# In one batch of a fused attention and channel MLP kernel, the x of two tiles made two slots later, behind the next batch's scores

## The chip, the cores and the metric

The kernel runs on one core of one Trainium2 chip. The metric is the device time of one execution in microseconds (us). The kernel before takes 257.06 us (median of 3 runs, 256.99 to 257.06). TensorE (PE) does the matmuls, VectorE (DVE) and ScalarE (ACT) empty the accumulators and do the element-wise work, GpSimd (POOL) makes some sums and issues loads. All runs told of here were in the fast state, with a granted TensorE clock of 0.99 to 1.00.

## The reference, cut to what matters

```python
a = softmax(phi)                      # 8 batches, 8 heads, 576 rows, 32 memories
k_m, v_m = a^T k, a^T v               # per head, 32 x 64
attn = softmax(q k_m^T / 8)
x  = (attn v_m), heads side by side   # 8 x 576 x 512
xn = (x - mean) / sqrt(var + 1e-6) * g_ln
out = x + relu(xn @ w_ch1) @ w_ch2    # w_ch1 512 x 2048, w_ch2 2048 x 512
```

The kernel doesn't normalise x before the first product. It multiplies w_ch1 with v_m once a batch ("w1b"), takes the mean out there, and applies 1/sqrt(var) ("rstd") at the very end. So x of a tile is needed only for its statistics and for the last addition, and there is some freedom as to when it is made.

## The kernel before

Two batches make a pair of 1152 rows, which is nine tiles of 128 rows. The even batch ends with tiles 0 to 3, the odd one with tiles 4 to 8. The parts that matter, shortened:

```python
def big(...):  return psum.tile(..., tag="big", bufs=3)     # three accumulators, in rotation
def one(...):  return psum.tile(..., tag="one", bufs=2)     # two accumulators: second product

def x_tiles(pr, ts):             # x of one or two tiles
    o_ps = big(...);             # matmuls from Eh and vb, 8 for tiles 6 and 7
    nc.scalar.activation(out=x, in_=o_ps, func=AF.Copy)              # ACT
    for i in range(n): bn_stats(x), bn_aggr -> mv                    # DVE

def x_rstd(pr, ts):
    rstd = Ln(var + eps); rstd = Exp(-0.5 * rstd)                    # ACT, waits for mv

def a_den(b, finish=True):       # denominators of the next batch's softmax
    den = big(...); matmuls; rd = Ln(den)                            # PE, ACT
    if finish: a_den2(b)         # rd = Exp(-rd) on ACT; Eh = E * rs * rd on DVE

def mm2(pr, t, j0, j1):          # second product of tile t, accumulator from one()
    ...
    if j1 == JC: mm2_out(pr, t)  # DVE: x = ch_ps * rstd + x; then the store

for b in range(1, B):
    mm1(b, 0, JC)                # h of this batch, 64 matmuls
    ex = {...}                   # slot 2i+half: what runs behind that half of tile i
    ...
    ex[1] += [lambda: a_tr(nb)]                    # kvT of the next batch
    ex[1] += [lambda: x_tiles(pr, t1)]             # t1 = tiles 6, 7 in an odd batch
    ex[2] += [a_sum(nb), a_w1b(nb, 0), a_w1b(nb, 1)]
    ex[2] += [lambda: x_rstd(pr, t1)]
    ex[3] += [lambda: a_sc(nb)]                    # scores of the next batch
    if odd: ex[4] += [lambda: x_tiles(pr, t2), lambda: x_rstd(pr, t2)]   # t2 = tile 8
    ex[3] += [a_vb(nb)]
    ex[4] += [a_den(nb)]
    ex[6 if odd else 5] += [a_w1b(nb, 2), a_w1b(nb, 3)]
    ...
    for i, t in enumerate(tiles):
        for half in range(2):
            mm2(pr, t, 8 * half, 8 * (half + 1))
            for f in ex[2 * i + half]: f()
```

The schedule is manual: each engine executes in the order in which the code names its instructions.

The softmax here doesn't subtract the row's maximum and nothing guards it: scores larger than these inputs give would overflow.

Of the kernel before, what the change touches and what calls it, by code (L numbers as in the profile page):

```python
# [16 lines left out]
def kernel(  # L17
# [38 lines left out]
    def big(shape, dtype, name):  # L56
        return psum.tile(shape, dtype, name=name, tag="big", bufs=3)
# [38 lines left out]
    def load(b):  # L96
        loaded[b] = (phis[b] if b > 2 else load_phi(b, nc.gpsimd), load_kv(b), load_q(b))
# [81 lines left out]
    def a_exp(b):  # L179
        phi_st, kv, q_bf = loaded[b]  # L180
        e = att.tile([P, NS, 4, M], BF16, name="e_sb")
        nc.scalar.activation(out=e.rearrange("p c j m -> p j c m"),  # L182
                             in_=phi_st.rearrange("p j (c m) -> p j c m", m=M), func=AF.Exp)
        st8[b] = {"e": e, "kv": kv, "q": q_bf}
        if b >= 2:
            es = att.tile([P, P], FP32, name="es")
            ev = e.rearrange("p c j m -> p c (j m)")
            a4 = att.tile([P, 4, P], FP32, name="es4", bufs=1)
            nc.gpsimd.tensor_tensor(out=a4, in0=ev[:, 0:4], in1=ev[:, 4:8], op=ALU.add)  # L189
            a2 = att.tile([P, 2, P], FP32, name="es2", bufs=1)  # L190
            nc.gpsimd.tensor_tensor(out=a2, in0=a4[:, 0:2], in1=a4[:, 2:4], op=ALU.add)
            nc.gpsimd.tensor_tensor(out=es, in0=a2[:, 0], in1=a2[:, 1], op=ALU.add)
            nc.gpsimd.tensor_tensor(out=es, in0=es, in1=ev[:, 8], op=ALU.add)
            hl = att.tile([P, 2, P], BF16, name="hl")
            nc.gpsimd.tensor_copy(out=hl[:, 0], in_=es)
            nc.gpsimd.tensor_tensor(out=hl[:, 1], in0=es, in1=hl[:, 0], op=ALU.subtract)
            st8[b]["es"] = hl
# [37 lines left out]
    def a_kv(b):  # L235
        ps = big([P, 2, 512], FP32, "kv_ps")
        kv_mm(b, ps, slice(0, 2))
        if b < 2:
            kv_sum(b, ps)
            rs_out(b, ps)  # L240
        k_out(b, ps, True)
        v_out(b, ps[:, :, D:2 * D])
# [59 lines left out]
    def a_sc(b):  # L302
        s = st8[b]
        kvT, qT = s["kvT"], s["qT"]
        E_ = att.tile([P, 2, 2 * HP], BF16, name="E_sb", bufs=1)
        for g in range(2):
            sc = big([P, 2, 512], FP32, "sc_ps")
            for j in range(4):
                for r in range(2):
                    nc.tensor.matmul(  # L310
                        sc[32 * j:32 * (j + 1), r, 0:HP],
                        kvT[64 * r:64 * (r + 1), g, 32 * j:32 * (j + 1)],
                        qT[64 * r:64 * (r + 1), j, :, TS * g:TS * (g + 1)],
                        start=True, stop=True, tile_position=(64 * r, 32 * j))
            nc.scalar.activation(out=E_[:, g].rearrange("p (a x) -> p a x", a=2),  # L315
                                 in_=sc[:, :, 0:HP], func=AF.Exp, scale=s["rs"][:, g:g + 1])
        s["E"] = E_
# [46 lines left out]
    def mm1(b, j0, j1):  # L364
        s = st8[b]
        if b % 2 == 0 and j0 == 0:
            pair[b // 2] = moe.tile([P, JC, 2 * S], BF16, name="rT", bufs=1)
        rT = pair[b // 2]
        off = S * (b % 2)
        for j in range(j0, j1):  # L370
            h_ps = big([P, 2, 512], FP32, "h_ps")
            for g in range(2):
                for half in range(2):
                    nc.tensor.matmul(  # L374
                        h_ps[:, half, 0:HS], s["w1b"][:, g, P * j:P * (j + 1)],
                        s["Eh"][:, g, HS * half:HS * (half + 1)],
                        start=(g == 0), stop=(g == 1))
            dst = rT[:, j, off:off + S].rearrange("p (a x) -> p a x", a=2)
            if j % 3 or j == 0:
                nc.scalar.activation(out=dst, in_=h_ps[:, :, 0:HS], func=AF.Relu)  # L380
            else:
                nc.vector.tensor_scalar(out=dst, in0=h_ps[:, :, 0:HS], scalar1=0.0, scalar2=None,  # L382
                                        op0=ALU.max)
# [3 lines left out]
    def x_tiles(pr, ts):  # L387
        n = len(ts)
        o_ps = big([P, 2, 512], FP32, "o_ps")
        for i, t in enumerate(ts):  # L390
            parts = []
            lo = P * t
            while lo < P * (t + 1):
                bb = lo // S
                hi = min(P * (t + 1), S * (bb + 1))
                parts.append((2 * pr + bb, lo - S * bb, hi - S * bb, lo - P * t))
                lo = hi
            for (b, a, z, po) in parts:
                s = st8[b]
                for g in range(2):  # L400
                    for u in range(2):
                        r = 64 * u
                        ov = o_ps[po:po + z - a, u, 256 * i:256 * (i + 1)]
                        nc.tensor.matmul(  # L404
                            ov.rearrange("p (j e d) -> p j e d", e=2, d=D)[:, :, g, :],
                            s["Eh"][r:r + 64, g, a:z],
                            s["vb"][r:r + 64, g, 2 * u:2 * (u + 1), :].rearrange("p j d -> p (j d)"),
                            start=True, stop=True, tile_position=(r, po))
        x = moe.tile([P, 2, C], FP32, name="x_sb", bufs=4)
        nc.scalar.activation(out=x[:, 0:n].rearrange("p i (u y) -> p i u y", u=2),  # L410
                             in_=o_ps.rearrange("p u (i y) -> p i u y", i=2)[:, 0:n],
                             func=AF.Copy)
        mv = moe.tile([P, 2, 2], FP32, name="mv", bufs=4)
        for i in range(n):
            stt = moe.tile([P, 6], FP32, name="bst", bufs=4)
            nc.vector.bn_stats(out=stt, in_=x[:, i, :])  # L416
            nc.vector.bn_aggr(out=mv[:, i, :], in_=stt)  # L417
        for i, t in enumerate(ts):
            xs[(pr, t)] = (x[:, i, :], mv, i, n)

    def x_rstd(pr, ts):
        _, mv, _, n = xs[(pr, ts[0])]
        rstd = moe.tile([P, 2], FP32, name="rstd", bufs=4)
        nc.scalar.activation(out=rstd[:, 0:n], in_=mv[:, 0:n, 1], func=AF.Ln, bias=eps_sb)  # L424
        nc.scalar.activation(out=rstd[:, 0:n], in_=rstd[:, 0:n], func=AF.Exp, scale=-0.5)
        for t in ts:
            x, _, i, _ = xs[(pr, t)]
            xs[(pr, t)] = (x, rstd[:, i:i + 1])
# [123 lines left out]
    for b in range(1, B):  # L552
        pr = b // 2
        mm1(b, 0, JC)
        odd = b % 2
        tiles = [4, 5, 6, 7, 8] if odd else [0, 1, 2, 3]
        t1, t2 = tiles[2:4], tiles[4:5]
        nb = b + 1
        if b > 1:
            x_rstd(pr, tiles[0:2])  # L560
        ex = {i: [] for i in range(2 * len(tiles))}
        if nb < B:
            ex[0] += [lambda: a_exp(nb), lambda: a_qT(nb, 0), lambda: a_kv(nb)]
            if nb + 1 < B:
                ex[0] += [lambda: phis.update({nb + 1: load_phi(nb + 1)})]
            ex[1] += [lambda: a_tr(nb)]
        if b == 1:
            ex[0] += [lambda: x_tiles(0, [4, 5]), lambda: x_rstd(0, [4, 5])]
        ex[1] += [lambda: x_tiles(pr, t1)]
        if nb < B:  # L570
            ex[2] += [lambda: a_sum(nb), lambda: a_w1b(nb, 0), lambda: a_w1b(nb, 1)]
        ex[2] += [lambda: x_rstd(pr, t1)]
        if nb < B:
            ex[3] += [lambda: a_sc(nb)]
        if odd:
            ex[4] += [lambda: x_tiles(pr, t2), lambda: x_rstd(pr, t2)]
        if nb < B:
            ex[3] += [lambda: a_vb(nb)]
            ex[4] += [lambda: a_den(nb)]
            ex[6 if odd else 5] += [lambda: a_w1b(nb, 2), lambda: a_w1b(nb, 3)]  # L580
            ex[8 if odd else 6] += [lambda: x_tiles(nb // 2, [4, 5] if nb % 2 else [0, 1])]
            if nb + 1 < B:
                ex[7] += [lambda: load(nb + 1)]
        for i, t in enumerate(tiles):
            if b == B - 1 and t == tiles[-1]:
                mm2_last(pr, t)
                continue
            for half in range(2):
                mm2(pr, t, 8 * half, 8 * (half + 1))
                for f in ex[2 * i + half]:  # L590
                    f()
# [30 lines left out]
```

## Time and profile before

| of the profile before (span 254.5 us) | value |
|---|---|
| PE busy | 95% of the span |
| DVE, ACT busy | 61%, 51% |
| batch 1, from the first kv matmul of batch 2 to the first h matmul of batch 2 | 64.11 to 85.67, 21.56 us |
| from there to the end of the span | 168.8 us |
| granted clock | 1.00 |

Busy shares are of recorded instructions, and the end of a matmul is modelled; so I read starts. Below, "the stretch" is the third row. It contains everything that the change moves. One record of a matmul can be missing: the profile before shows seven of the eight second products that open the stage, so I don't start the stretch there. In the timeline the columns are start, duration, engine and line, out<-in, shapes, count, and in brackets the idle time of the engine before it and who ended it.

### The profile page before, as it was taken

Reading aid. Unit: us, or ns where it says so; the run is one execution under the profiler, and the core shown is the slowest. Engines: PE = TensorE matmul, PEld = TensorE weight load, DVE = VectorE, ACT = ScalarE, POOL = GpSimd, SP = SyncE. Lnnn points to the kernel's source line nnn. Section 1 sums busy time; section 2 is a strip of 40 time slices with the busy share of each in tenths; the row PEclk is TensorE's granted clock in tenths of the full one; section 3 lists DMA queues with packets and bytes.
Section 4 is the critical chain, followed back from the end, with each engine's and each line's share of the span. In section 5 each row is a group of like instructions: output and inputs, shape, how many; then the busy total and the mean of one; then the engine's idle time right before and its main releaser. Section 6 shows DMA issues by size and latency. Waiting matters only on the chain.

```text
span 254.5 us, 5778 instructions
## 1 busy us (share of the span) xinstructions
PE 241.0 (95%) x2422; PEld 131.6 (52%) x2453; DVE 155.0 (61%) x306; ACT 129.1 (51%) x219; POOL 51.8 (20%) x87
## 2 busy tenths in 40 slices
PE   7978999899999999999999999999999999999994
PEld 2534555457434665457444664466544764466453
DVE  3346763684486845695486737684568638683431
ACT  3165662668444582648343672558253663565210
POOL 8633330000900009000710018000900022000000
PEclk9999999999999999999999999999999999999999
DMA  7999999999497492988399483969398541130133
GB/s 157 196 207 207 206 255 231 267 183 159 89 208 148 95 213 44 205 174 152 109 173 204 90 195 56 215 140 175 90 202 177 112 76 41 45 78 5 44 82 82
DMA packets 41922, 36.82 MB, mean 145 GB/s; under 512 B 17444, under 2 KB 37160, under 8 KB 41896
## 3 DMA queue, kind: packets, MB, share of 16 engines
q0 software_dynamic: 17248, 19.53, 45.2%
q1 hardware_dynamic: 24488, 16.79, 28.9%
q8 instruction: 19, 0.31, 0.5%
q10 hardware_dynamic: 160, 0.13, 0.2%
q14 instruction: 7, 0.06, 0.1%
HBM read 41.42 MB, written 9.44 MB: 200 GB/s over the span
## 4 chain that ended last, share of the span: by engine, by line
PE 76%; DMA 17%; DVE 3%; issue 2%; ACT 1%; POOL 1%; POOLq 0%
PE ch_ps L438 42%; PE h_ps L374 22%; DMA q_bf<-in_q_dram 7%; DMA w2b<-in_moe_w_ch_dram 6%; DMA kv_bf<-in_k_dram 3%; PE w1b_ps L353 3%; PE o_ps L404 2%; PE kv_ps L205 2%; PE den_ps L327 2%; PE last_ps L450 1%; PE sc_ps L310 1%; DVE bst L416 1%; POOL q_bf L92 1%; DVE w1b L357 1%; ACT x_sb L410 0%
## 5 line engine op out<-in xcount | busy, mean ns | idle before, releaser
L438 PE MATMUL ch_ps<-w2b,rT 128*128 128x512 bf16 x531 | 125.9, 380 | 2.2 <-issue 1.3
L438 PEld LDWEIGHTS <-rT 128*128 128x128 bf16 x560 | 51.3, 98 | 62.3 <-issue 6.7
L374 PE MATMUL h_ps<-Eh,w1b 128*128 128x288 bf16 x512 | 67.1, 285 | 0.7 <-ACT rT L380 0.5
L380 ACT ACTIVATE rT<-h_ps 128x576 bf16<-128x576 f32 x88 | 52.6, 648 | 21.3 <-PE h_ps L374 21.1
L374 PEld LDWEIGHTS <-w1b 128*128 128x128 bf16 x512 | 49.6, 97 | 17.8 <-issue 2.6
L357 DVE SCALAR_TENSOR_TENSOR w1b<-m_sb,rsum,w1b_ps 128x512 bf16<-128x512 f32 x64 | 43.6, 739 | 4.2 <-ACT m_sb L169 2.6
L382 DVE TENSOR_SCALAR rT<-h_ps 128x576 bf16<-128x576 f32 x40 | 30.3, 757 | 24.0 <-PE h_ps L374 23.9
L410 ACT ACTIVATE x_sb<-o_ps 128x1024 f32<-128x1024 f32 (+1 forms) x20 | 18.6, 937 | 37.8 <-PE o_ps L404 36.5
L462 DVE SCALAR_TENSOR_TENSOR x_sb<-ch_ps,rstd,x_sb 128x512 f32<-128x512 f32 x35 | 26.1, 745 | 15.0 <-PE ch_ps L438 14.4
L189 POOL TENSOR_TENSOR es<-e_sb 128x512 f32<-128x512 bf16 x6 | 6.9, 1149 | 137.9 <-ACT e_sb L182 137.9
L416 DVE BATCH_NORM_STATS2 bst<-x_sb 128x6 f32<-128x512 f32 x36 | 24.4, 677 | 8.1 <-ACT x_sb L410 8.1
L339 DVE SCALAR_TENSOR_TENSOR Eh<-E_sb,rs,rden 128x576 bf16<-128x576 bf16 x16 | 12.4, 814 | 14.1 <-ACT rden L338 14.1
L315 ACT ACTIVATE E_sb<-sc_ps,rs 128x640 bf16<-128x640 f32 x16 | 11.9, 790 | 11.6 <-PE sc_ps L310 11.6
L424 ACT ACTIVATE rstd<-mv,eps_sb 128x2 f32<-128x2 f32 (+1 forms) x20 | 5.9, 296 | 20.3 <-DVE mv L417 20.3
L353 PE MATMUL w1b_ps<-w1r,kvT 64*32 64x512 bf16 x256 | 10.8, 383 | 0.8 <-DVE kvT L258 0.4
L227 DVE CAST v<-kv_ps 128x128 bf16<-128x128 f32 x8 | 2.3, 290 | 14.7 <-ACT k L220 13.7
L174 PE MATMUL w_ps<-fill 128*128 128x512 f32 x14 | 9.7, 814 | 1.6 <-DVE fill L119 1.6
L329 ACT ACTIVATE rden<-den_ps 128x576 f32<-128x576 f32 x16 | 9.5, 644 | 2.7 <-PE den_ps L327 2.7
L182 ACT ACTIVATE e_sb<-phi_st 128x1152 bf16<-128x1152 f32 x8 | 9.2, 1151 | 2.7 <-DMA phi_st<-in_phi_dram 2.7
L338 ACT ACTIVATE rden<-rden 128x576 f32<-128x576 f32 x16 | 10.0, 681 | 0.0
L205 PEld LDWEIGHTS <-e_sb 64*32 64x32 bf16 x648 | 6.3, 90 | 5.0 <-ACT e_sb L182 3.0
L92 POOL DMA_DIRECT2D q_bf<-in_q_dram x10 | 7.6, 757 | 4.6 <-DMA w2b<-in_moe_w_ch_dram 1.9
(69 smaller groups left out, 143.6 us busy)
## 6 DMA issues: line engine op xcount, KB each, us to landing
out_dram<-x_sb SPq DMA_DIRECT2D x70, 128.0 KB, 2.5
kv_bf<-in_k_dram POOLq DMA_DIRECT2D x7, 576.0 KB, 7.0
kv_bf<-in_v_dram POOLq DMA_DIRECT2D x7, 576.0 KB, 9.4
phi_st<-in_phi_dram SPq DMA_DIRECT2D x6, 576.0 KB, 4.7
q_bf<-in_q_dram POOLq DMA_DIRECT2D x6, 576.0 KB, 11.9
w1r<-in_moe_w_ch_dram POOLq DMA_DIRECT2D x4, 512.0 KB, 12.9
w2b<-in_moe_w_ch_dram POOLq DMA_DIRECT2D x4, 512.0 KB, 18.9
q_bf<-in_q_dram POOLq DMA_DIRECT2D x4, 288.0 KB, 11.9
```

Source lines behind the costliest of these rows:

```text
L205: nc.tensor.matmul(ps[32 * j:32 * (j + 1), g, 0:D * (sl.stop - sl.start)], e[r:r + TS, c, j, :], kv[r:r + TS, j, sl, D * c:D * (c + 1)], s ...
L315: nc.scalar.activation(out=E_[:, g].rearrange("p (a x) -> p a x", a=2), in_=sc[:, :, 0:HP], func=AF.Exp, scale=s["rs"][:, g:g + 1])
L339: nc.vector.scalar_tensor_tensor(out=Eh[:, g, :], in0=s["E"][:, g, 0:S], scalar=s["rs"][:, g:g + 1], in1=rd[:, g].rearrange("p a x -> p (a ...
L353: nc.tensor.matmul(ps[32 * j:32 * (j + 1), g, :], s["kvT"][r:r + 64, 2, 32 * j:32 * (j + 1)], w1r[r:r + 64, j, fs], start=True, stop=True, ...
L357: nc.vector.scalar_tensor_tensor(out=s["w1b"][:, g, fs], in0=m_sb[:, fs], scalar=s["rsum"][:, g:g + 1], in1=ps[:, g, :], op0=ALU.mult, op1 ...
L374: nc.tensor.matmul(h_ps[:, half, 0:HS], s["w1b"][:, g, P * j:P * (j + 1)], s["Eh"][:, g, HS * half:HS * (half + 1)], start=(g == 0), stop= ...
L380: nc.scalar.activation(out=dst, in_=h_ps[:, :, 0:HS], func=AF.Relu)
L382: nc.vector.tensor_scalar(out=dst, in0=h_ps[:, :, 0:HS], scalar1=0.0, scalar2=None, op0=ALU.max)
L410: nc.scalar.activation(out=x[:, 0:n].rearrange("p i (u y) -> p i u y", u=2), in_=o_ps.rearrange("p u (i y) -> p i u y", i=2)[:, 0:n], func ...
L416: nc.vector.bn_stats(out=stt, in_=x[:, i, :])
L438: nc.tensor.matmul(ch_ps, rT[:, j, P * t:P * (t + 1)], w2b[:, j, :], start=(j == 0), stop=(j == JC - 1))
L462: nc.vector.scalar_tensor_tensor(out=x, in0=ch_ps, scalar=rstd, in1=x, op0=ALU.mult, op1=ALU.add)
```

## The change

The intent is to take the 8 matmuls of tiles 6 and 7 out of the way of batch 2's w1b and scores, where TensorE has its two visible waits. Only batch 1 is changed.

```diff
-        ex[1] += [lambda: x_tiles(pr, t1)]
+        if b > 1:
+            ex[1] += [lambda: x_tiles(pr, t1)]
         if nb < B:
             ex[2] += [lambda: a_sum(nb), lambda: a_w1b(nb, 0), lambda: a_w1b(nb, 1)]
-        ex[2] += [lambda: x_rstd(pr, t1)]
+        if b > 1:
+            ex[2] += [lambda: x_rstd(pr, t1)]
         if nb < B:
             ex[3] += [lambda: a_sc(nb)]
+        if b == 1:
+            ex[3] += [lambda: x_tiles(pr, t1), lambda: x_rstd(pr, t1)]
```

## The prediction

> **What bounds the kernel now.** I read the page's first part, then the busy times per stage, then the order of events inside the one stage that the change touches. Engines and occupancy first:
>
> ```profile
> PE 241.0 (95%) x2422; PEld 131.6 (52%) x2453; DVE 155.0 (61%) x306; ACT 129.1 (51%) x219; POOL 51.8 (20%) x87
> ```
>
> TensorE is busy 95% of the span, at full granted clock in every slice, and 76% of the chain that ended last is PE. Inside the loop over batches the time of a stage is therefore what TensorE has to do plus the gaps in which it waits. Each batch has its h products (mm1), then a stage of "second products" of x tiles with the preparation of the next batch put between them in slots. The change touches batch 1's stage alone. Its busy times, against those of batches 2, 3 and 5 (length of stretch, then busy time of each engine):
>
> ```profile
> 62.17:85.46 23.29, 22.03 (x240) 10.08 (x241) 16.03 (x33) 10.77 (x19) 6.00 (x10) 1.00 0.71 138
> 93.50:111.90 18.40, 18.07 (x213) 8.30 (x215) 12.43 (x25) 8.69 (x15) 6.00 (x10) 1.00 0.82 163
> 119.90:141.70 21.80, 21.37 (x228) 9.75 (x230) 14.49 (x29) 9.66 (x18) 6.00 (x10) 1.00 0.76 147
> 176.10:197.90 21.80, 21.38 (x227) 9.76 (x230) 14.46 (x29) 9.70 (x18) 5.99 (x10) 1.00 0.78 156
> ```
>
> Batches 1, 3 and 5 have five tiles each. Batch 1's stage takes 23.29 us against 21.80, because it also makes x of tiles 4 and 5 itself (12 matmuls, 0.53 us of PE, 1.02 us of ACT, 1.7 us of DVE) and because TensorE idles 23.29-22.03 = 1.26 us in it against 21.80-21.37 = 0.43 us. So the most that any reordering of this stage can win is about 1.26-0.43 = 0.83 us, 0.3% of 257. Where the gaps are, from the timeline by engine (start, duration, what, and in brackets the idle time with its releaser):
>
> ```profile
> 68.77 0.75 DVE L462 SCALAR_TENSOR_TENSOR x_sb<-ch_ps,rstd,x_sb 128x512 f32<-128x512 f32 x1 [0.60 <-ACT rstd L425]
> 69.97 0.63 PE L353 MATMUL w1b_ps<-w1r,kvT 64*32 64x512 bf16 x16 [0.41 <-DVE kvT L258]
> 71.69 2.70 DVE L357 SCALAR_TENSOR_TENSOR w1b<-m_sb,rsum,w1b_ps 128x512 bf16<-128x512 f32 x4
> 73.13 0.33 PE L310 MATMUL sc_ps<-qT,kvT 64*32 64x320 bf16 x8 [0.44 <-DVE w1b L357]
> 75.55 0.60 ACT L410 ACTIVATE x_sb<-o_ps 128x512 f32<-128x512 f32 x1 [1.23 <-DMA out_dram<-x_sb]
> 76.18 0.69 DVE L416 BATCH_NORM_STATS2 bst<-x_sb 128x6 f32<-128x512 f32 x1 [0.73 <-ACT x_sb L410]
> 77.13 0.29 ACT L424 ACTIVATE rstd<-mv,eps_sb 128x1 f32<-128x1 f32 x1 [0.98 <-DVE mv L417]
> 77.56 1.17 ACT L329 ACTIVATE rden<-den_ps 128x576 f32<-128x576 f32 x2
> 78.62 1.25 ACT L338 ACTIVATE rden<-rden 128x576 f32<-128x576 f32 x2
> 79.34 1.55 DVE L339 SCALAR_TENSOR_TENSOR Eh<-E_sb,rs,rden 128x576 bf16<-128x576 bf16 x2 [2.25 <-ACT rden L338]
> 80.05 3.63 PE L438 MATMUL ch_ps<-w2b,rT 128*128 128x512 bf16 x16
> 80.80 0.75 DVE L462 SCALAR_TENSOR_TENSOR x_sb<-ch_ps,rstd,x_sb 128x512 f32<-128x512 f32 x1
> ```
>
> The reader is to see two gaps of PE, 0.41 us until kvT is copied and 0.44 us until the first w1b accumulator has been emptied, and then the chain that has no gap on PE yet but little room: ACT's log of the denominators (77.56), its exponentials (78.62), DVE's Eh (79.34) and, behind Eh in DVE's order, the output of tile 6 (80.80 to 81.55). The accumulators of the second product are two ("one", bufs=2), so tile 8 needs the one of tile 6. Tile 8's first matmul is the ninth of the sixteen that start at 80.05; they go at 3.56/16 = 0.2225 us, so it starts at about 81.83, only 0.28 us after tile 6's output has ended.
>
> **What the Trainium skill says.** "PSUM — Partial Sum Buffer", section "Engine vs sequencer instructions", states that the queues of ScalarE and VectorE are strict FIFO and that matmuls start in program order. The trace agrees: the denominators were in PSUM at 76.10 (75.44+0.66), yet ACT stood 0.98 us until 77.13 for the variance of tile 8, which is before them in its order. "Perfetto Trace Analysis", section "Optimization Strategy", says to find the gaps of the contended engine and what releases them, and that repeated bubbles can mean too few PSUM or SBUF buffers; the 0.44 us gap is of that kind (a rotation of three "big" accumulators). The same page, "Optimizing Scalar/DVE Operations", warns that engines which are not saturated can still cause bubbles on others. ACT at 51% and DVE at 61% are that here.
>
> **The change part by part.** No instruction is added or removed; the order of both built programs shows the same counts. For batch 1 alone, "x of tiles 6, 7" moves:
> - on PE: 8 matmuls (67.31 to about 67.64, 0.33 us of stream) from before tile 5's first half to after batch 2's scores;
> - on ACT: the 1.01 us copy and two small activations (0.29+0.20) from before the scores' exponentials to after them, but before the copy of tile 8's x and before the logs of the denominators;
> - on DVE: two statistics pairs (1.70 us) from before the w1b outputs to after them and after tile 5's output.
>
> The rotation of "big" shifts too: scores take the buffers of the sum and of w1b part 0, and o_ps of tiles 6, 7 takes that of w1b part 1.
>
> (1) Before the w1b products: PE is 0.33 us earlier at 69.4, but the kvT copies that it then needs stand on DVE behind tile 4's output, which waits for tile 4's rstd until 68.77, all unchanged. So w1b still starts at 69.97. Gain 0; the 0.41 us gap becomes 0.74.
>
> (2) Scores: DVE loses 1.70 us of statistics in front of the w1b outputs; these now start when part 0 is in PSUM, 69.97+0.41 = 70.4 instead of 71.69, and end at 70.4+2.7 = 73.1 instead of 74.39. The buffer of part 0 comes free at about 71.8, before the scores start at 72.36, so the 0.44 us gap goes.
>
> (3) o_ps of 6, 7 now stands behind the scores (ready about 72.8) and needs w1b part 1 emptied: 73.1 plus 0.08. It costs a wait of 0.35 and its 0.33 us. Tile 6's first half starts at 73.5 instead of 73.39. Sum of (1) to (3): about +0.1 us, no gain.
>
> (4) ACT: exponentials of the scores 72.76 to 74.24 (1.48 for two, as batch 3 shows), then the copy of x 6, 7 at 74.16 to 75.18. DVE is free (w1b and tile 5's output end at 73.8), so the statistics go 75.22 to 76.92, rstd starts at 76.96, and ACT comes to the copy of tile 8's x at 76.96+0.43 = 77.39 instead of 75.55. From there the spacings of the trace hold: statistics of tile 8 at 78.02, its rstd at 78.97, logs at 79.40 (77.56 before: +1.84 us), exponentials and Eh likewise, tile 6's output at 79.40+(80.80-77.56) = 82.64, done at 83.39.
>
> (5) PE: w1b part 3 may wait 0.3 us for the first log, which is hidden by the next. Tile 8 is ready at 81.83+0.1 but must wait for tile 6's accumulator until 83.39+0.06 = 83.45. Against 81.83 before, that is **+1.6 us**, of which 1.5 us is a new gap. What follows keeps its spacing: w1b parts 2 and 3 are emptied by DVE from 83.3 to 86.0, and h of batch 2 starts at 85.67+1.6 = 87.3, so no second wait is added; DVE's first h output comes at 89.4 and DVE is done with tile 8's output at about 89.2.
>
> From batch 2 on the program is unchanged and TensorE bound, no load is waited for by PE in it, and there is no slack to take the delay up. Sum: 257.06+1.6 = 258.66, and I set 258.6.
>
> **Rivals.** (a) The intended gain: both gaps of PE shrink, up to 0.83 us, 256.2 to 256.7. For it speaks that the 0.44 us gap really goes; against it that the DVE chain to kvT does not move, and that o_ps meets a buffer wait of equal size. It would need step (4) to be hidden as well. (b) Nothing: (1) to (3) cancel and the delay of ACT is absorbed, 257.0 to 257.3. For it: PE need not wait for ACT anywhere in 75 to 82 before. Against: the room is 0.28 us and the delay 1.84 us; ACT would have to be over 1.5 us earlier than I count. (c) More: the late w1b outputs on DVE, 86.0 instead of 84.2, push batch 2's first h outputs or the statistics of its tiles 0, 1 and stall the three "big" buffers; 259 to 260. Against: those users shift by the same 1.6 us. (d) The output transfers move with tile 6's output. The copy of tile 8's x names such a transfer as its releaser, but in truth its o_ps ended at 75.51; x buffers are four and the reused one was stored long before. I give it 0.1 us at most.
>
> **Range and chances.** The steps are spacings read from the same trace, each good to 0.05 to 0.1 us, and the total hangs on step (5). If DVE starts the w1b outputs 0.2 us later or earlier, PE's new wait hardly moves, as ACT's chain hangs on the scores' start at 72.36. I take 257.6 to 259.3: the lower end has half of the delay absorbed, the upper one adds (c). A change of 2% is 5.1 us, three times the delay; a faster run by 2% is excluded by the 0.83 us bound. Chances: faster 0.01, same 0.97, slower 0.02.
>
> **What would show it.** In the profile after: the 0.44 us gap at the scores gone; kvT's wait at about 0.7 us; a short wait of o_ps of 6, 7 for w1b; ACT's logs at about 79.4; a new PE gap of about 1.5 us at 82 to 83.5 in front of tile 8's first matmul, released by DVE's output of tile 6; h of batch 2 at about 87.3; later stages unchanged in length. Wrong would be: batch 2's h products starting at or before 85.7, a gap at another place, or later stages of another length.

## The result, and the profile after

The changed kernel takes 258.62 us (median of 4, 258.34 to 258.71), the kernel before 257.02 us beside it. The ratio is 1.0061, with a 95% interval of 1.0044 to 1.0079. A ratio is the mean time of one kernel's fast runs over that of the other's in the same rounds, so it is not quite the ratio of the medians. The predicted time was 258.6 us.

The busy line of the page, and the stretches by engine (limits, length, then busy time and count of PE, PEld, DVE, ACT, POOL, then clock, DMA share and GB/s):

```profile
PE 240.8 (94%) x2422; PEld 131.8 (51%) x2453; DVE 155.0 (60%) x306; ACT 128.9 (50%) x219; POOL 52.0 (20%) x87
...
64.74:87.99 23.25, 20.47 (x232) 9.39 (x235) 15.70 (x32) 9.10 (x17) 5.71 (x10) 1.00 0.65 128
```

The same stretch of the kernel before:

```profile
64.11:85.67 21.56, 20.36 (x231) 9.39 (x234) 15.48 (x32) 9.22 (x17) 5.70 (x10) 1.00 0.71 138
```

The work of every engine is nearly the same (PE has one record and 0.11 us more). The stretch is 1.69 us longer, and 1.58 us of that is PE idle: 23.25-20.47 = 2.78 us instead of 21.56-20.36 = 1.20 us. Of these idle times 0.16 us before and 0.32 us after stand where a record is missing. Behind it nothing differs: from the first h matmul to the end it is 168.81 us (168.83 before).

The span itself is 2.3 us longer, more than the timed difference. The rest is not of the change: the kv matmul that opens the stretch started 0.63 us later in this profile, in front of any instruction that the change moves. TensorE's waits for w1r at the start, by the timeline, added up to 1.34 us before (0.50 and 0.84) and 2.21 us after (0.26, 1.15 and 0.80); all its waits for loads up to there were 2.22 and 3.04 us. In the eleven profiles that opening kv matmul starts between 64.11 and 65.21 us, whatever the kernel. The profile before is also of a fast execution, 256.29 us, below all of its timed runs (256.90 to 257.06).

The timeline of the changed kernel by engine, the rows that answer to those of the prediction (subtract 0.63 us to compare):

```profile
69.40 0.75 DVE L462 SCALAR_TENSOR_TENSOR x_sb<-ch_ps,rstd,x_sb 128x512 f32<-128x512 f32 x1 [0.60 <-ACT rstd L425]
70.60 0.62 PE L353 MATMUL w1b_ps<-w1r,kvT 64*32 64x512 bf16 x16 [0.85 <-DVE kvT L258]
71.08 2.72 DVE L357 SCALAR_TENSOR_TENSOR w1b<-m_sb,rsum,w1b_ps 128x512 bf16<-128x512 f32 x4 [0.27 <-PE w1b_ps L353]
72.99 0.47 PE L310 MATMUL sc_ps<-qT,kvT 64*32 64x320 bf16 x16
73.39 1.48 ACT L315 ACTIVATE E_sb<-sc_ps,rs 128x640 bf16<-128x640 f32 x2 [4.03 <-PE sc_ps L310]
73.86 0.40 PE L404 MATMUL o_ps<-vb,Eh 64*128 64x128 bf16 x8 [0.41 <-DVE w1b L357]
74.76 1.02 ACT L410 ACTIVATE x_sb<-o_ps 128x1024 f32<-128x1024 f32 x1
77.56 0.29 ACT L424 ACTIVATE rstd<-mv,eps_sb 128x2 f32<-128x2 f32 x1 [1.77 <-DVE mv L417]
78.05 0.60 ACT L410 ACTIVATE x_sb<-o_ps 128x512 f32<-128x512 f32 x1
79.63 0.29 ACT L424 ACTIVATE rstd<-mv,eps_sb 128x1 f32<-128x1 f32 x1 [0.98 <-DVE mv L417]
80.06 1.17 ACT L329 ACTIVATE rden<-den_ps 128x576 f32<-128x576 f32 x2
81.84 1.55 DVE L339 SCALAR_TENSOR_TENSOR Eh<-E_sb,rs,rden 128x576 bf16<-128x576 bf16 x2 [2.25 <-ACT rden L338]
83.31 0.74 DVE L462 SCALAR_TENSOR_TENSOR x_sb<-ch_ps,rstd,x_sb 128x512 f32<-128x512 f32 x1
84.10 1.89 PE L438 MATMUL ch_ps<-w2b,rT 128*128 128x512 bf16 x8 [1.11 <-DVE x_sb L462]
```

The scores now run as one group of 16 without their wait, as intended. But the wait for kvT has become 0.85 us, o_ps waits 0.41 us for a buffer, and ACT stands 1.77 us for the variances of tiles 6 and 7 and then 0.98 us for that of tile 8 before it comes to the logs (L329). The last row is the new gap: tile 8's second product waits 1.11 us for the output of tile 6 on DVE. The chain that ended last (`--critical`) runs in this window from the scores' exponentials at 73.39 to tile 6's output, done at 84.06, through ACT and DVE alone, and then to tile 8's matmuls. Before, it is on PE alone from the second half of the scores (73.13) on.

### The profile page after: what moved, and what is told of

The parts are those of the page before. It is cut to its first block, busy times and chain, and to the rows that moved or that the text cites. A ratio compares the mean times of both kernels' runs of the same rounds, so it can differ in the third digit from the quotient of the medians.

```text
span 256.8 us, 5779 instructions
## 1 busy us (share of the span) xinstructions
PE 240.8 (94%) x2422; PEld 131.8 (51%) x2453; DVE 155.0 (60%) x306; ACT 128.9 (50%) x219; POOL 52.0 (20%) x87
## 4 chain that ended last, share of the span: by engine, by line
PE 80%; DMA 6%; ACT 4%; DVE 4%; POOL 2%; issue 2%; ACTq 0%; POOLq 0%
PE ch_ps L438 43%; PE h_ps L374 24%; DMA w1r<-in_moe_w_ch_dram 6%; PE w1b_ps L353 3%; PE o_ps L404 2%; PE kv_ps L205 2%; PE last_ps L450 1%; PE den_ps L327 1%; DVE bst L416 1%; ACT E_sb L315 1%; POOL kv_bf L84 1%; PE sc_ps L310 1%; ACT x_sb L410 1%; POOL q_bf L92 1%; POOL w1r L137 1%
## 5 line engine op out<-in xcount | busy, mean ns | idle before, releaser
L329 ACT ACTIVATE rden<-den_ps 128x576 f32<-128x576 f32 x16 | 9.5, 644 | 2.6 <-PE den_ps L327 2.6
```

## The experiments

The theory: ACT and DVE work in a fixed order; the statistics of tiles 6, 7 and 8, one after the other, hold up the logs of the denominators; Eh is late by that; the output of tile 6, which stands behind Eh on DVE, is late; tile 8 waits for tile 6's accumulator. Rival A: it is Eh itself, the copies or the buffers. Rival B: the loss is TensorE's own new waits before the scores and at o_ps. The rivals are told apart by what a repair at one link leaves over. All kernels gave correct results. In this table the times are medians of 6 runs, the ratio is against the kernel before in the same rounds, and "stretch less before" is the length of the stretch minus 21.56 us:

| run | time us | ratio, 95% interval | stretch | stretch less before | gap before tile 8 |
|---|---|---|---|---|---|
| changed (4 runs) | 258.62 | 1.0061, 1.0044 to 1.0079 | 23.25 | +1.69 | 1.11 |
| e1_out6_before_eh | 257.55 | 1.0029, 1.0012 to 1.0046 | 21.98 | +0.42 | none |
| e2_rstd_behind_den | 257.34 | 1.0012, 0.9997 to 1.0026 | 21.74 | +0.18 | none |
| e3_rstd67_behind_x8 | 257.55 | 1.0020, 1.0005 to 1.0035 | 22.38 | +0.82 | 0.48 |
| e4_after_kvt_first | 257.82 | 1.0030, 1.0016 to 1.0044 | 22.33 | +0.77 | 1.12 |
| e5_before_kvt_first | 256.68 | 1.0002, 0.9983 to 1.0021 | 21.23 | -0.33 | none |
| e7_kvt_first_rstd_behind | 256.58 | 0.9998, 0.9977 to 1.0020 | 20.82 | -0.74 | none |
| e6_best | 255.59 | 0.9959, 0.9942 to 0.9977 | 20.45 | -1.11 | none |
| e8_changed_again | 258.75 | 1.0062, 1.0042 to 1.0082 | 23.26 | +1.70 | 1.11 |
| e9_both_repairs_again | 255.86 | 0.9963, 0.9944 to 0.9981 | 20.82 | -0.74 | none |

The kernel before had medians of 257.01 (with e1 to e4), 256.75 (e5 to e7) and 256.79 (e8, e9). In every one of these profiles the time from the first h matmul to the end is 168.8 to 169.0 us, so a stretch passes into the span whole. The expectations of e1 to e4 count the stretch from the first recorded second product, 23.16 us before; because of the missing record I compare their differences: an expected 23.5 is +0.34.

### Tile 6's output ahead of Eh

```diff
-            ex[4] += [lambda: a_den(nb)]
+            ex[4] += [lambda: a_den(nb, finish=b > 1)]
+            if b == 1:
+                ex[5] += [lambda: a_den2(nb)]
```

> The changed kernel, with tile 6's output put ahead of batch 2's two Eh products in VectorE's order (the exponentials of the denominators and Eh move behind tile 6's second half); ScalarE's logs stay late. I measure the stretch from the first second-product matmul of tile 4 to the first h matmul of batch 2: before 62.51 to 85.67 = 23.16 us, changed 63.13 to 87.99 = 24.86 us. Theory (tile 8 waits for tile 6's accumulator, which VectorE gives back only behind Eh): the gap of 1.1 us before tile 8 goes, though the logs are still at about 79.4; left over are the 0.17 us of the o_ps wait and the 0.24 us wait of w1b part 3: stretch 23.5 to 23.7, time 257.4. Rival A (it is Eh itself, late for x of the next batch and for h): stretch stays at 24.6 or more, 258.5. Rival B (the loss is TensorE's own new waits before the scores and at o_ps of tiles 6 and 7): stays at 24.8, 258.6.

Measured: +0.42 us of stretch (+0.34 to +0.54 expected). The rows of DVE and PE in this run:

```profile
79.43 0.72 DVE L462 SCALAR_TENSOR_TENSOR x_sb<-ch_ps,rstd,x_sb 128x512 f32<-128x512 f32 x1
81.77 1.55 DVE L339 SCALAR_TENSOR_TENSOR Eh<-E_sb,rs,rden 128x576 bf16<-128x576 bf16 x2 [1.61 <-ACT rden L338]
...
80.22 0.86 PE L353 MATMUL w1b_ps<-w1r,kvT 64*32 64x512 bf16 x16
81.01 3.63 PE L438 MATMUL ch_ps<-w2b,rT 128*128 128x512 bf16 x16
```

Eh is as late as in the changed kernel (81.77 against 81.84, with the stretch beginning 0.08 us earlier), and still tiles 7 and 8 run through as one group of 16. So a late Eh costs nothing by itself; it costs through what stands behind it on DVE. That is against rival A's first form and against rival B, which would have left +1.7. The timed median lies 0.54 us over the kernel before and the interval (0.3 to 1.2 us) holds the 0.42. What is left over shows in w1b: its 16 matmuls take 0.86 us instead of 0.62, because the accumulator of part 3 is that of the first denominators and comes free only behind the late first log; in e2 and e3, with earlier logs, it is 0.62 again.

### Both rstd behind the denominators

```diff
-            ex[3] += [lambda: x_tiles(pr, t1), lambda: x_rstd(pr, t1)]
+            ex[3] += [lambda: x_tiles(pr, t1)]
...
-            ex[4] += [lambda: x_tiles(pr, t2), lambda: x_rstd(pr, t2)]
+            ex[4] += [lambda: x_tiles(pr, t2)]
+            if b > 1:
+                ex[4] += [lambda: x_rstd(pr, t2)]
             ex[4] += [lambda: a_den(nb)]
+            if b == 1:
+                ex[4] += [lambda: x_rstd(pr, t1), lambda: x_rstd(pr, t2)]
```

> The changed kernel, with the rstd activations of tiles 6, 7 and of tile 8 moved behind batch 2's logs and exponentials of the denominators on ScalarE; TensorE's and VectorE's order as in the changed kernel. Theory (ScalarE in its fixed order stands for two variances, one after the other, before it comes to the logs): logs about 3.2 us earlier than in the changed kernel (2.5 us after the end of the scores' exponentials or less), no gap before tile 8: stretch 23.3 to 23.5, time 257.1 to 257.3. Rival A (the copies on ScalarE or the buffers are the cause): gap before tile 8 stays over 0.5 us, 258 or more. Rival B (TensorE's own waits): 24.8, 258.6.

Measured: +0.18 us of stretch (+0.14 to +0.34 expected), no gap before tile 8. From ACT's rows:

```profile
73.86 1.48 ACT L315 ACTIVATE E_sb<-sc_ps,rs 128x640 bf16<-128x640 f32 x2 [4.02 <-PE sc_ps L310]
75.23 1.02 ACT L410 ACTIVATE x_sb<-o_ps 128x1024 f32<-128x1024 f32 x1
76.82 0.60 ACT L410 ACTIVATE x_sb<-o_ps 128x512 f32<-128x512 f32 x1 [0.57 <-PE o_ps L404]
77.32 1.19 ACT L329 ACTIVATE rden<-den_ps 128x576 f32<-128x576 f32 x2
```

The logs start 77.32-73.86 = 3.46 us behind the scores' exponentials, in the changed kernel 80.06-73.39 = 6.67 us: 3.21 us earlier, as expected. Both copies and the rotation of buffers are as in the changed kernel, so they are not what made tile 8 wait; the two waits for variances are. The 0.18 us is what the change does at and before the scores, seen alone.

### A middle dose

```diff
-            ex[3] += [lambda: x_tiles(pr, t1), lambda: x_rstd(pr, t1)]
+            ex[3] += [lambda: x_tiles(pr, t1)]
...
-            ex[4] += [lambda: x_tiles(pr, t2), lambda: x_rstd(pr, t2)]
+            ex[4] += [lambda: x_tiles(pr, t2)]
+            if b == 1:
+                ex[4] += [lambda: x_rstd(pr, t1)]
+            ex[4] += [lambda: x_rstd(pr, t2)]
```

> A middle dose: the changed kernel with only the rstd of tiles 6, 7 moved behind the copy of tile 8's x on ScalarE, still ahead of the logs. The copy of tile 8's x then doesn't wait for the statistics of tiles 6 and 7; VectorE still does all three statistics (about 3.0 us from the end of the copy of x 6, 7) before the logs. Theory: logs 0.6 us earlier than in the changed kernel, so tile 8 also: gap before tile 8 about 0.5 instead of 1.1 us, stretch 24.2 to 24.3, time 257.9 to 258.1. Rival A (a threshold effect of buffers, not the length of the chain): either 24.8 or 23.5, nothing between. Rival B: 24.8, 258.6.

Measured: the gap before tile 8 was 0.48 us, as expected, with these rows:

```profile
73.42 1.48 ACT L315 ACTIVATE E_sb<-sc_ps,rs 128x640 bf16<-128x640 f32 x2 [4.03 <-PE sc_ps L310]
79.22 1.17 ACT L329 ACTIVATE rden<-den_ps 128x576 f32<-128x576 f32 x2
83.26 1.89 PE L438 MATMUL ch_ps<-w2b,rT 128*128 128x512 bf16 x8 [0.48 <-DVE x_sb L462]
```

The stretch was +0.82 us, where +1.04 to +1.14 was expected, and the time 257.55 us, below the expected 257.9. One thing was mis-sized. The logs came 5.80 us behind the scores' exponentials (79.22-73.42), so 0.87 us earlier than in the changed kernel and not 0.6, and the stretch is shorter by just that (23.25-22.38). The gap shrank by only 0.63 us of it: the earlier logs also freed the accumulator of w1b part 3, so its wait of 0.24 us went too, and tile 8 was ready earlier by as much. The result lies between the ends, as a chain's length does and a threshold would not.

### kvT ahead of tile 4's output

```diff
             ex[1] += [lambda: a_tr(nb)]
+            if b == 1:
+                ex[1] += [lambda: mm2_out(pr, tiles[0])]
...
-                mm2(pr, t, 8 * half, 8 * (half + 1))
+                mm2(pr, t, 8 * half, 8 * (half + 1), finish=b > 1 or i > 0)
```

> The changed kernel, with tile 4's output put behind batch 2's kvT copies on VectorE, so that the copies no longer wait for tile 4's rstd. Theory: the 0.85 us wait of the w1b matmuls for kvT falls under 0.15; everything behind it, ScalarE's chain from the scores included, moves forward together by about 0.7 us; the gap before tile 8 stays at about 1.1: stretch 24.1 to 24.2, time 257.9. Rival (the wait for kvT is idle time that the later gap before tile 8 hides anyway): gap before tile 8 grows by 0.7 and the stretch stays at 24.8, 258.6.

Measured: +0.77 us of stretch, 0.92 us less than the changed kernel; expected was 0.66 to 0.76 less. The time of 257.82 us is near the expected 257.9. The gap before tile 8 did not grow, it stayed at 1.12 us, so the rival falls: the whole chain to tile 8 hangs on the scores and moves with them. The gain was a little larger because w1b had no wait at all. The row of tile 8:

```profile
83.28 1.89 PE L438 MATMUL ch_ps<-w2b,rT 128*128 128x512 bf16 x8 [1.12 <-DVE x_sb L462]
```

### The same in the kernel before

The same edit as the one above, made in the kernel before.

> The kernel before (x of tiles 6 and 7 at its old place), with tile 4's output put behind batch 2's kvT copies on VectorE. From here on I measure from the first kv matmul of the stage (first record of kv_ps) to the first h matmul of batch 2: before 64.11 to 85.67 = 21.56 us, changed 23.25. Theory: w1b starts 0.48 us earlier, the statistics of tiles 6 and 7 still stand ahead of the w1b outputs on VectorE and hang on ScalarE's copy, so the scores' second wait grows by about 0.2: stretch 21.3, 0.25 us less than before, time 256.8. Rival (the two gaps of TensorE are independent): 21.08, 0.48 less, 256.5.

Measured: -0.33 us of stretch (-0.26 expected; the rival said -0.48). The scores' second half waited longer for w1b, as the theory says:

```profile
73.54 0.33 PE L310 MATMUL sc_ps<-qT,kvT 64*32 64x320 bf16 x8 [0.59 <-DVE w1b L357]
```

The wait grew from 0.44 to 0.59 us (the theory said by about 0.2), so the two gaps are not independent: the statistics of tiles 6 and 7 stand between them on DVE. The stretch lies nearer to the theory than to the rival. In time the run is the same as before (1.0002), and an effect of 0.33 us, 0.13%, is below what the interval can show.

### Both repairs on the changed kernel

The edits of e2 and of e4 together.

> The changed kernel with both repairs: kvT copies ahead of tile 4's output on VectorE, and both rstd behind the logs and exponentials on ScalarE. Theory (the two are in series: the first takes 0.77 to 0.91 us out of the way to the scores, the second takes the new gap away): stretch of 21.56+0.18-0.85 = about 20.9, 0.65 us less than before; time 256.4. So the gain that the change was after is there once kvT does not wait. Rival (something else, like the statistics on VectorE, takes up the time): stretch 21.5 to 21.8, 257.0 to 257.2.

> The same kernel as e7_kvt_first_rstd_behind, whose trace showed a stretch of 20.82 us (0.74 less than before) but whose times gave a ratio of 0.9998 with an interval of 0.9977 to 1.0020, just short of the 0.9971 that 0.74 us would be. If the stretch alone counts, the stretch is 20.8 again and the ratio between 0.996 and 0.998. If something outside the stretch gives the gain back (a rival: loads or outputs that collide later), the time from h to the end is over 168.9 us in this profile and the ratio stays at 1.000.

Measured: the stretch was 20.82 us both times, -0.74 us. The times of e7 did not show it (0.9998), those of e9 did (0.9963, with an interval that leaves out 1). The time from h to the end was 168.86 and 168.79 us, so nothing outside the stretch gives the gain back. I take the first as scatter of the start, in front of the stretch. That is argued, not shown: only one execution of each run has a trace, and e7's was the fastest of its six (255.85 us of 255.85 to 257.52). The waits for loads that TensorE's rows name in front of the stretch, 1.36 to 3.54 us in the eleven profiles, tend to be longer where the stretch begins later, but do not settle it (e9: 1.36 us and a begin at 64.69; before: 2.22 us and 64.11). The changed kernel, run in the same rounds as e9, repeated its stretch and its ratio:

> The changed kernel itself, beside the next run on one chip. Stretch from the first kv matmul of the stage to the first h matmul of batch 2: 23.25 us again (before 21.56). The rest, from h to the end, 168.8 us in every profile so far, and the prologue up to the first kv matmul between 64.1 and 65.2 us (loads), so the span alone decides nothing below 1 us. Time: 1.5 to 1.7 us over the kernel before.

### A version that beats both

The edit of e4 in the changed kernel, and for batch 1:

```diff
-            ex[3] += [lambda: x_tiles(pr, t1), lambda: x_rstd(pr, t1)]
...
-        if odd:
+        if odd and b > 1:
             ex[4] += [lambda: x_tiles(pr, t2), lambda: x_rstd(pr, t2)]
             ex[4] += [lambda: a_den(nb)]
+            if b == 1:
+                ex[4] += [lambda: x_tiles(pr, t1), lambda: x_rstd(pr, t1)]
+                ex[5] += [lambda: x_tiles(pr, t2), lambda: x_rstd(pr, t2)]
```

> A version meant to beat both: kvT copies ahead of tile 4's output; x of tiles 6 and 7 behind batch 2's denominators (not behind its scores), and x of tile 8 behind tile 6's second half, so that the o_ps of tiles 6, 7 does not wait for a w1b accumulator and ScalarE does the logs before the copies. Theory: no wait of TensorE left between the kv matmuls and h, stretch 20.5 to 20.8, 0.8 to 1.0 us less than before; time 256.0 to 256.3. Rival (the tile 6 output on VectorE, which now waits for the late rstd of tiles 6, 7, holds up tile 8 again): a gap before tile 8 of 0.5 or more, stretch 21.2 or more.

Measured: -1.11 us of stretch, slightly more than expected, and 255.59 us, 0.4% under the kernel before. The stretch, by engine:

```profile
64.64:85.09 20.45, 20.45 (x234) 9.23 (x234) 15.07 (x32) 9.21 (x17) 5.69 (x10) 1.00 0.75 150
```

TensorE is busy in all of it. ACT still stands 1.77 us for the variances of tiles 6 and 7, but now it has done the logs before:

```profile
74.56 1.19 ACT L329 ACTIVATE rden<-den_ps 128x576 f32<-128x576 f32 x2 [0.70 <-PE den_ps L327]
...
79.58 0.30 ACT L424 ACTIVATE rstd<-mv,eps_sb 128x2 f32<-128x2 f32 x1 [1.77 <-DVE mv L417]
```

The output of tile 6 is then at 80.14 us and tile 8 is not held up. So the wait for a variance costs only by what stands behind it.

## Why the prediction was right or wrong

The time was right, and so was the path to it. That it agrees to 0.02 us is luck: the same kernel had a median of 258.75 us in e8, and the interval of the ratio allows 1.1 to 2.0 us of loss. The path is the better test. In the times of the profile after less 0.63 us:

- Step (1), no gain before w1b: right. The w1b matmuls start at 69.97 us, as before. The gap is 0.85 and not 0.74, because o_ps had taken a little more of TensorE's time than its 0.33 us.
- Step (2), the scores' wait goes: right. DVE starts the w1b outputs at 70.45 (70.4 predicted).
- Step (3), o_ps waits for w1b part 1: right, 0.41 us where 0.35 was said. Steps (1) to (3) together were put at +0.1 us; run e2 shows +0.18 us.
- Step (4), the logs at 79.40: measured 79.43. Shown by e2 and e3 to be the cause.
- Step (5), tile 8 at 83.45: measured 83.47, against 81.83 before. Its split was off. I put 1.5 us of the 1.6 at tile 8 and called w1b part 3's wait of 0.3 us hidden. In the trace w1b takes 0.24 us longer, and the gap at tile 8 is 1.11 us as recorded, or 1.23 us from start to start (84.10 less 81.09 and eight spacings of 0.2225). The sum is the same, since tile 8 waits to a fixed moment; but e1 shows that the part 3 wait does count as soon as tile 8's own gap is gone.
- The rest of the kernel "no slack to take the delay up": right, 168.81 against 168.83 us.

One reading was loose. The prediction counts the 0.44 us gap among the bubbles that, by the skill, can mean too few buffers; the skill speaks there of a gap that repeats. TensorE did wait for an accumulator, but this wait of the scores for w1b is the only one in the profile before, and in the changed kernel it went with the same three accumulators, since DVE did the w1b outputs before the statistics (from 70.45 instead of 71.69 us).

Of the rivals, (a) gave too small a bound. I took batch 3's 0.43 us of PE idle as a floor, and so 0.83 us as the most a reordering could win. Run e6 won 1.11 us of the 1.20 us that PE idled in this stretch: the idle time of a sister stage is not a floor. Rival (b), absorbed by slack, had the right measure, 0.28 us of room, and failed for the reason given. Rivals (c) and (d) left no trace.

The change's aim was not empty: e7 and e9 show 0.74 us less with the same place of o_ps, once kvT is not behind tile 4's output and rstd not in front of the logs. Not all of that is the change's: the kvT edit alone gives 0.33 us (e5), so the new place of o_ps, with the rstd moved, adds 21.23-20.82 = 0.41 us to it, and without the kvT edit it still loses 0.18 us (e2). It failed since it moved three engines' work by moving one call, and two of the three came to lie in front of something that another engine waited for: ACT's rstd in front of the logs, and DVE's statistics of tiles 6 and 7 in front of those of tile 8.

## What to carry to other kernels

When one call issues work on several engines, find for each engine what the call now stands in front of, and compare the delay with the room at the place where the busiest engine next needs it; here the logs were 79.43-77.56 = 1.87 us late (1.84 predicted), and the room was 0.28 us. Split such a call, so that the short operations that wait for other engines (rstd here) stand behind those that others wait for. And look at what a gap hangs on before taking work out from in front of it: the kvT wait only grew, from 0.41 to 0.85 us, when TensorE came to it earlier.

## What the Trainium skill lacked or had wrong

- "Perfetto Trace Analysis", section "Optimization Strategy", sends the reader to the gaps of the contended engine. It lacks the counterpart, the room of the chains that have no gap yet: 0.28 us before tile 8, which no gap in the profile before shows, turned the removal of a 0.44 us gap into 1.69 us of loss.
- "PSUM — Partial Sum Buffer", section "Engine vs sequencer instructions", states the strict FIFO of ScalarE and VectorE, and the runs agree. It does not say that an accumulator's release is delayed by everything ahead of its reader: with Eh ahead of tile 6's output TensorE waited 1.11 us, and with their order exchanged not at all, though Eh was as late.
- No page that I used says how much the start of a kernel, in which TensorE waits for loads, varies between executions: the first kv matmul of the stage began at 64.11 to 65.21 us in eleven profiles, taken on several chips, with the same instructions in front of it. Differences under 1 us were to be read from a stretch, not from the span.
